# A list scheduler that orders an attention and two-layer MLP kernel: waiting for urgent tasks, later stores and loads, later squares

## The chip, the cores and the metric

The kernel runs on one core of one Trainium2 chip. The metric is the device time of one execution in microseconds (us). A core has TensorE (matrix products; PE in the rows, with PEld for its weight loads), VectorE (DVE), ScalarE (ACT), GpSimd (POOL) and SyncE (SP). Here GpSimd issues the stores of intermediate results, and SyncE issues all loads and the stores of the output. Each engine runs its own instructions strictly in the order in which they were issued to it when the program was built, and waits on semaphores for the others.

## The reference

```python
def reference(q, k, v, phi, moe_w_in, moe_w_out, moe2_w_in, moe2_w_out):
    a = exp(phi - phi.max(2)); a /= a.sum(2) + 1e-9        # 8 batches, 8 heads, 576 tokens, 32 slots
    k_m, v_m = einsum('bhsm,bhsd->bhmd', a, k), einsum('bhsm,bhsd->bhmd', a, v)
    s = q @ k_m.T / sqrt(64); p = exp(s - s.max(-1)); p /= p.sum(-1) + 1e-9
    x = (p @ v_m).transpose(0, 2, 1, 3).reshape(4608, 512)
    h = x @ moe_w_in;  x = (h * sigmoid(h)) @ moe_w_out    # 512 -> 2048 -> 512
    h = x @ moe2_w_in; return where(h > 0, h, exp(min(h, 0)) - 1) @ moe2_w_out
```

All inputs and the output are float32. q, k, v and phi are 8 x 8 x 576 x 64 (phi: x 32).

## The kernel before, in words

A float32 product is made of three float16 products: an operand is split into a high part (`split_hi`, line 170, ScalarE) and a low part (`split_lo`, line 175, VectorE). Products of the two-layer parts use a seven-product scheme for 2 x 2 blocks, so that sums of quarter matrices are formed on VectorE before and after (lines 134 and 1461). Weights arrive as 64-bit words ("raw", 1 MB a load, line 305), are converted in five steps (line 311 on ScalarE, then four on VectorE), split, and written back to memory as float16 (tile `hl_q`, stores `w1os`, `w2is`, `w2os` on GpSimd's queue, lines 444 and 448); later they are read again as `w1s`, `wi` and `wq`.

The program has three parts. The **first**, up to 77 us, is a written-out list (`FIRST`) of the attention of batches 0 and 1. **Plan 1** (`plan_first`, 77 to 718 us) holds the first MLP for batches 0 to 7, with the attention of later batches and the preparation of the second MLP's weights beneath it. In it a batch's silu `h <- ph` (line 1106, ScalarE) follows products `ph <- aT,u`; h is split into `T` and multiplied as `ph <- T,w1s`; `y` is the batch's result, stored to `x2d` (line 1277, 576 KB) and squared and summed by ScalarE (line 354) for a scale. **Plan 2** (718 us to the end) finishes batch 7 and runs the second MLP over 9 blocks of 512 tokens: products `h2A` and `h2D`, ScalarE's copies `h <- h2A` (line 1457), VectorE's additions (line 1461), elu (lines 1492, 1495 and 1499), the split into `t`, and products `o <- t,wq`.

The order inside plan 1 and plan 2 is made by a list scheduler, `Plan`. Each task has an engine, a cost, a rank (lower is more urgent) and dependencies. `run` simulates the engines greedily: the engine that can start earliest takes, of the tasks that are ready by then, the one of lowest rank, and its code is issued at that moment. The costs and the simulated time decide this order and nothing else; on the chip no engine waits for anything but semaphores. In plan 1 the ranks are due times worked out backwards from the products (`by_due`, in us of the planner); in plan 2 they are numbers written by hand, 1000 for each block. `store` gives a GpSimd store a cost of 4.0 + KB/200, and `load` gives a DMA load 3.6 + KB/350 in plan 1 and 2.2 + KB/350 in plan 2, with a term `late` where a caller adds one. `ring` and `take` tell the scheduler which buffers a task must wait for. The raw loads, `hl_q` pairs and scratch tiles share one ring of two buffers, so a raw load or a split can also wait for a store that reads the buffer it wants.

The scheduler's simulation starts a task as soon as nothing ready is more urgent:

```python
start = max(free[eng], min(at[i] for i in r))
i = min((i for i in r if at[i] <= start), key=lambda i: (self.tasks[i][2], i))
```

In plan 2 the last batch's `plan_out1` returns a list `done`, on which the gate for opening the output's PSUM tiles (`open_ps_o`) and the scale of the last batch (`x2_scales(B - 1, NB)` in block 2) both wait.

Of the kernel before, what the change touches and what calls it, by code (L numbers as in the profile page):

```python
# [10 lines left out]
F32 = mybir.dt.float32  # L11
# [8 lines left out]
P = 128  # L20
# [6 lines left out]
HS = S // 2  # L27
# [12 lines left out]
NY = 2  # L40
NT = 3
KVLATE, QLATE = 1.0, 3.0
NKV = 3
W2FROM, W2TO, AHEAD = 0.2, 0.95, 35
SHIFT = 9
# [45 lines left out]
def attn_moe_moe(ctx: ExitStack, tc: tile.TileContext, qT, phiT, kvm, kvt, w1i, w1o, w2i, w2o, out):  # L91
# [96 lines left out]
    class Plan:  # L188
# [47 lines left out]

        def store(self, kb, rank, fn, deps=()):

            return self.add("POOL", 4.0 + kb / 200, rank, fn, deps, 1.2)

        def ring(self, name, n):

# [8 lines left out]
        def run(self):  # L251
            if self.ahead is not None:
                self.by_due()
            n = len(self.tasks)
            left = [len(t[4]) for t in self.tasks]
            users = [[] for _ in range(n)]
            for i, t in enumerate(self.tasks):
                for d in t[4]:
                    users[d].append(i)
            at = [0.0] * n  # L260
            ready = {}
            free = {}
            for i, t in enumerate(self.tasks):
                ready.setdefault(t[0], [])
                free[t[0]] = self.busy.get(t[0], 0.0)
                if not left[i]:
                    ready[t[0]].append(i)
            order = []
            while len(order) < n:
                best = None  # L270
                for eng, r in ready.items():
                    if not r:
                        continue
                    start = max(free[eng], min(at[i] for i in r))
                    i = min((i for i in r if at[i] <= start), key=lambda i: (self.tasks[i][2], i))
                    if best is None or start < best[0]:
                        best = (start, eng, i)
                start, eng, i = best
                ready[eng].remove(i)
                order.append(i)  # L280
                _, cost, _, fn, _, hold = self.tasks[i]
                end = start + cost
                free[eng] = start + hold
                for u in users[i]:
                    at[u] = max(at[u], end + (0.0 if self.tasks[u][0] == eng else COST["wait"]))
                    left[u] -= 1
                    if not left[u]:
                        ready[self.tasks[u][0]].append(u)
                fn()
            return {e: max(0.0, free[e] - free["PE"]) for e in free}  # L290
# [10 lines left out]
    def load64(src, f, s, tag=None):  # L301

        shape = list(src.shape[2:])
        t = (late if tag else two).tile([P, shape[1], shape[2], 2], U32, tag=tag or "raw", name="raw")
        nc.sync.dma_start(out=t.rearrange("p a b w -> p a (b w)"), in_=src[f, s].bitcast(U32))
        raw[id(src), f, s] = t
# [234 lines left out]
    def plan_quads(pl, due, src, e, shape, s_all, n_all, p_all, part, store):  # L541
# [7 lines left out]
        ready, free = {}, {}  # L549
        for k, name in enumerate(order):  # L550
            pl.due = due[k]
            load = pl.load(1024, 0, lambda k=k: load64(src, e, k), pl.ring("raw", 2))
            rfree = pl.take("raw", load)

            def alloc(name=name):
                t[name] = two.tile([P, *shape], F32, tag="stage", name="quad", bufs=4)
                return t[name]

            ready[name] = plan_convert(pl, 0, alloc, src, e, k, [load] + pl.ring("stage", 4))
            free[name] = pl.take("stage", ready[name])  # L560
            rfree.append(ready[name])
# [619 lines left out]
        pl.take("wr", t)  # L1181
        return t

    def plan_out1(pl, b, r, silus, made, stored, scales, y_tile, y_ring):

# [87 lines left out]
        for e in E:  # L1275
            def store(e=e):
                nc.gpsimd.dma_start(out=x2d[b][:, e::2], in_=w[e]["y"].rearrange("p (a t) s -> p a (t s)", a=2))

            def squares(e=e):
                sumsq(mx_x2[:, b, e:e + 1], w[e]["y"], w[e]["y"])  # L1280

            t = pl.store(590, r - 2500, store, [c11[e], c12[e], c21[e], c22[e]])
            yfree[e].append(pl.add("ACT", act(4 * HS), r - 100, squares, [t]))
            done += [yfree[e][-1], c12[e], c21[e], p3[e]]
        return done, [loads[j][0] for j in WSEQ]


    FIRST4, LAST3 = (0, 5, 4, 2), (1, 6, 3)
# [476 lines left out]
    with tc.manual_schedule():  # L1765
# [15 lines left out]
        last["made"] = {}  # L1781
        for n in range(NT):
            last["T_free", n] = pl.take("T", None)
        out1, loads = plan_out1(
            pl, B - 1, 0, None, NT, {}, [], lambda: ph2.tile([P, 4, HS], F32, tag="y", name="y", bufs=2), ("y", 2))
        w1s_load = pl.gates["x"] = loads[4:5]
        pl.gates[1] = [pl.add("PE", 0.0, 0, open_ps_o, out1)]
        for n in range(4, 7):
# [5 lines left out]
        for i in range(NB):  # L1794
            for q in range(KQ):
                plan_in2(pl, i, q)
            plan_out2(pl, i, 0)
            if i == 2:
                pl.add("DVE", 2.5, 1000 * i + RANK["x2"], lambda: x2_scales(B - 1, NB), [y[i]["t_done", KQ - 1, 0]] + out1)
            if i + 1 < NB:  # L1800
                plan_x2(pl, i + 1, 1000 * i + RANK["x2"])
            plan_out2(pl, i, 1)
# [50 lines left out]
```

## Time and profile before

| | us |
|---|---|
| Median of three runs (lowest, highest) | 1409.9 (1408.24, 1411.55) |
| The profiled execution | 1407.48 |
| Its span | 1405.5 |
| TensorE busy with matmuls | 1354.2 (96%) |
| VectorE busy | 1127.9 (80%) |
| ScalarE busy | 951.1 (68%) |
| Mean granted TensorE clock | 0.989 of full speed |

The span runs from the first to the last instruction; the execution takes about 2 us more. Busy shares are means over stages that differ. In a timeline row a bracket such as [3.08 <-ACT pad L178] says how long the engine was idle before the instruction and which work, by engine, tile and line, released it. A name such as SPq or POOLq means the engine's DMA queue. The granted clock is a share of the full 2.4 GHz.

### The profile page before, as it was taken

How to read it: one execution, taken by the hardware profiler on the slowest of the kernel's cores; microseconds unless marked ns; L12 is line 12 of the kernel's file. 1: busy time of each engine (PE TensorE's matmuls, PEld its weight loads, DVE VectorE, ACT ScalarE, POOL GpSimd, SP SyncE). 2: the span in 40 equal slices, each digit the busy share in tenths (PEclk: the TensorE clock that was granted, in tenths of full speed). 3: DMA queues.
4: the chain of work that ended last, by engine and by line, in shares of the span. 5: the costliest groups of instructions: out<-in, count | busy, mean ns of one | idle time of the engine just before them, and what ended most of it. 6: DMA issues, size and time to landing. Idle time of an engine off the chain costs nothing.

```text
span 1405.5 us, 28627 instructions
## 1 busy us (share of the span) xinstructions
PE 1354.2 (96%) x12048; PEld 1092.9 (78%) x12048; DVE 1127.9 (80%) x1753; ACT 951.1 (68%) x1357; POOL 51.1 (4%) x85
## 2 busy tenths in 40 slices
PE   4999999999989999999998999999999999999998
PEld 2667676776756767676786888888888888888887
DVE  6889788796977989797767787887879787878784
ACT  3667765957857596776657576767667676767583
POOL 0001100000010010011000000000000000000000
PEclk8999999999999999999999999999999999999999
DMA  9565767367475657736293233332424151514130
GB/s 363 178 227 176 287 246 255 140 218 278 150 246 197 232 188 253 257 129 224 104 369 132 83 112 107 110 109 84 135 69 151 43 177 43 163 56 136 57 120 31
DMA packets 68801, 233.06 MB, mean 166 GB/s; under 512 B 9025, under 2 KB 15169, under 8 KB 64065
## 3 DMA queue, kind: packets, MB, share of 16 engines
q1 hardware_dynamic: 60288, 199.78, 42.1%
q0 software_dynamic: 8384, 31.46, 5.6%
q8 instruction: 94, 1.54, 0.4%
q14 instruction: 35, 0.28, 0.1%
HBM read 186.12 MB, written 40.89 MB: 162 GB/s over the span
## 4 chain that ended last, share of the span: by engine, by line
PE 79%; DMA 7%; DVE 4%; issue 4%; ACT 4%; POOL 0%; SPq 0%; ACTq 0%; POOLq 0%; DVEq 0%
PE ph L1020 24%; PE o L1020 22%; PE h2A L1020 12%; PE h2D L1020 9%; PE ph L1069 4%; DMA wi<-w2is 3%; PE ph L1027 2%; PE sc L775 2%; PE up L860 2%; PE kvp L679 1%; DMA kv<-in_kvm 1%; DMA x2d<-y 1%; DMA raw<-in_w2i 1%; DMA w2is<-hl_q 1%; DVE T L175 1%
## 5 line engine op out<-in xcount | busy, mean ns | idle before, releaser
L1020 PE MATMUL o<-t,wq 128*128 128x256 f16 x3024 | 361.4, 273 | 1.3 <-DVE t L175 1.3
L1020 PEld LDWEIGHTS <-wi 128*128 128x128 f16 x3024 | 296.2, 98 | 50.1 <-issue 7.2
L1020 PEld LDWEIGHTS <-wq 128*128 128x128 f16 x3024 | 296.1, 98 | 36.3 <-issue 1.7
L1020 PE MATMUL ph<-T,w1s 128*128 128x288 f16 x2352 | 301.9, 286 | 0.0
L1020 PEld LDWEIGHTS <-w1s 128*128 128x128 f16 x2352 | 225.9, 98 | 64.7 <-issue 8.6
L1020 PE MATMUL h2A<-xh,wi 128*128 128x256 f16 x1728 | 228.2, 274 | 10.0 <-ACT h L1457 6.0
L1457 ACT ACTIVATE h<-h2A,inv 128x256 f32<-128x256 f32 x288 | 133.3, 467 | 111.7 <-PE h2A L1020 108.9
L1020 PE MATMUL ph<-aT,u 128*128 128x288 f16 x1344 | 179.8, 290 | 8.8 <-ACT h L1106 8.5
L1020 PEld LDWEIGHTS <-u 128*128 128x128 f16 x1344 | 129.0, 99 | 59.2 <-issue 26.4
L170 ACT ACTIVATE t<-h,s_g 128x768 f16<-128x768 f32 (+1 forms) x144 | 147.4, 1037 | 37.5 <-DVE h L1499 25.9
L1020 PE MATMUL h2D<-xh,wi 128*128 128x256 f16 x1296 | 172.0, 274 | 0.1
L175 DVE SCALAR_TENSOR_TENSOR t<-h,s_g,t 128x768 f16<-128x768 f32 (+1 forms) x144 | 163.4, 1145 | 4.9 <-ACT t L170 4.9
L175 DVE SCALAR_TENSOR_TENSOR T<-h,c,T 128x1152 f16<-128x1152 f32 x98 | 137.2, 1412 | 22.7 <-ACT T L170 22.6
L1461 DVE SCALAR_TENSOR_TENSOR h<-h2D,inv,h 128x256 f32<-128x256 f32 x216 | 102.4, 480 | 65.1 <-PE h2D L1020 43.8
L170 ACT ACTIVATE T<-h,c 128x1152 f16<-128x1152 f32 x98 | 119.9, 1253 | 25.1 <-DVE h L134 19.9
L134 DVE TENSOR_TENSOR h<-h 128x256 f32<-128x256 f32 (+1 forms) x302 | 128.5, 463 | 3.0
L1499 DVE SCALAR_TENSOR_TENSOR h<-e,h 128x1024 f32<-128x1024 f32 x72 | 87.9, 1221 | 20.7 <-ACT e L1495 20.2
L1106 ACT ACTIVATE h<-ph,inv 128x576 f32<-128x576 f32 x112 | 82.1, 737 | 15.9 <-PE ph L1020 15.4
L1492 ACT ACTIVATE e<-h 128x1024 f32<-128x1024 f32 x72 | 75.5, 1048 | 13.7 <-DVE h L1461 13.6
L1495 ACT ACTIVATE e<-e 128x1024 f32<-128x1024 f32 x72 | 75.7, 1051 | 1.0
L1069 PE MATMUL ph<-h,w1o 128*128 128x288 f32 x256 | 66.7, 416 | 0.0
L134 DVE TENSOR_TENSOR h<-h,h 128x1152 f32<-128x1152 f32 x42 | 56.5, 1353 | 7.2 <-ACT h L1106 7.0
(183 smaller groups left out, 1271.2 us busy)
## 6 DMA issues: line engine op xcount, KB each, us to landing
w1s<-w1os SPq DMA_DIRECT2D x98, 512.0 KB, 4.5
wi<-w2is SPq DMA_DIRECT2D x56, 896.0 KB, 4.7
kv<-in_kvm SPq DMA_DIRECT2D x48, 256.0 KB, 5.5
q<-in_qT SPq DMA_DIRECT2D x32, 288.0 KB, 7.3
out<-ye SPq DMA_DIRECT2D x36, 256.0 KB, 2.0
raw<-in_w1i SPq DMA_DIRECT2D x8, 1024.0 KB, 11.5
raw<-in_w1o SPq DMA_DIRECT2D x8, 1024.0 KB, 4.9
raw<-in_w2i SPq DMA_DIRECT2D x8, 1024.0 KB, 6.7
```

What stands on the lines that cost most here:

```text
L134: nc.vector.tensor_tensor(out=out, in0=a, in1=b, op=op)
L170: nc.scalar.activation(out=hi, in_=x, func=AF.Copy, scale=s)
L175: nc.vector.scalar_tensor_tensor(out=lo, in0=x, scalar=s, in1=hi, op0=ALU.mult, op1=ALU.subtract)
L775: nc.tensor.matmul(ps[o:o + 64, c // 2, 2 * p:2 * p + 2], z["q", p][:, t0:t0 + 64], z["kT"][:, p // 2, 64 * (p % 2):64 * (p % 2) + 64], st ...
L1020: nc.tensor.matmul(o, w, x[:, c], start=first, stop=last, **how)
L1069: nc.tensor.matmul(z[d][1][t], wB[d][:, k], h[k // KQ][:, t, k % KQ], start=(k == 0), stop=(k == KF - 1))
L1106: nc.scalar.activation(out=h[m // KQ][:, :, m % KQ], in_=w.pop(m), func=AF.Silu, scale=z["inv1"][:, m // 4:m // 4 + 1])
L1457: nc.scalar.activation(out=w["x"][:, s], in_=w["A"], func=AF.Copy, scale=inv)
L1461: return pl.add("DVE", COST["add"], base, lambda: nc.vector.scalar_tensor_tensor(out=w["x"][:, s], in0=w["D"], scalar=inv, in1=w["x"][:, s ...
L1492: nc.scalar.activation(out=w["e"], in_=w["x"][:, B21:], func=AF.Relu, scale=-1.0)
L1495: nc.scalar.activation(out=w["e"], in_=w["e"], func=AF.Exp, scale=-1.0)
L1499: nc.vector.scalar_tensor_tensor(out=x, in0=w["e"], scalar=-1.0, in1=x, op0=ALU.add, op1=ALU.max)
```

## The change

Three things change, all in the scheduler's numbers and rules; the set of instructions of every engine stays the same, and so does the written-out first part.

1. In `run`, for ScalarE and VectorE, if a task that is more urgent by over 10 (plan 1, us of due time) or over 50 (plan 2, ranks) becomes ready within SOON = 0.4 us of the simulated start, and the task otherwise chosen would still be running 0.2 us past that moment, the engine takes the urgent one and is idle until then. This holds in the simulation. On the chip it only means that the urgent instruction is issued ahead of the other.
2. In plan 1 a store is simulated as 6.0 + KB/200 in place of 4.0 + KB/200, and the raw loads of `plan_quads` (second MLP's weights) land 2.0 us later in the simulation.
3. The squares of the last batch's `y` get rank 1200 in plan 2 (they had -100, ahead of all of the second MLP), no longer stand in `done`, and are waited for only by the scale of the last batch in block 2.

```diff
+RAWLATE, STORE = 2.0, 6.0
+SOON, EARLIER = 0.4, 10.0
...
         def store(self, kb, rank, fn, deps=()):
-            return self.add("POOL", 4.0 + kb / 200, rank, fn, deps, 1.2)
+            return self.add("POOL", (4.0 if self.ahead is None else STORE) + kb / 200, rank, fn, deps, 1.2)
...
                     i = min((i for i in r if at[i] <= start), key=lambda i: (self.tasks[i][2], i))
+                    if eng in ("ACT", "DVE"):
+
+                        rank, end = self.tasks[i][2], start + self.tasks[i][1]
+                        soon = [k for k in r if start < at[k] <= start + SOON and end > at[k] + SOON / 2 and self.tasks[k][2] < rank - (EARLIER if self.ahead is not None else 50)]
+                        if soon:
+                            i = min(soon, key=lambda k: (at[k], k))
+                            start = at[i]
...
-            load = pl.load(1024, 0, lambda k=k: load64(src, e, k), pl.ring("raw", 2))
+            load = pl.load(1024, 0, lambda k=k: load64(src, e, k), pl.ring("raw", 2), RAWLATE)
...
-    def plan_out1(pl, b, r, silus, made, stored, scales, y_tile, y_ring):
+    def plan_out1(pl, b, r, silus, made, stored, scales, y_tile, y_ring, squares_rank=0):
...
-            yfree[e].append(pl.add("ACT", act(4 * HS), r - 100, squares, [t]))
-            done += [yfree[e][-1], c12[e], c21[e], p3[e]]
-        return done, [loads[j][0] for j in WSEQ]
+            yfree[e].append(pl.add("ACT", act(4 * HS), squares_rank, squares, [t]))
+            done += [c12[e], c21[e], p3[e]]
+        return done, [y[-1] for y in yfree], [loads[j][0] for j in WSEQ]
...
-        out1, loads = plan_out1(
-            pl, B - 1, 0, None, NT, {}, [], lambda: ph2.tile([P, 4, HS], F32, tag="y", name="y", bufs=2), ("y", 2))
+        out1, squares, loads = plan_out1(
+            pl, B - 1, 0, None, NT, {}, [], lambda: ph2.tile([P, 4, HS], F32, tag="y", name="y", bufs=2), ("y", 2), 1200)
...
-                pl.add("DVE", 2.5, 1000 * i + RANK["x2"], lambda: x2_scales(B - 1, NB), [y[i]["t_done", KQ - 1, 0]] + out1)
+                pl.add("DVE", 2.5, 1000 * i + RANK["x2"], lambda: x2_scales(B - 1, NB), [y[i]["t_done", KQ - 1, 0]] + squares)
```

Since costs and rules changed, the order of plan 1 and plan 2 is drawn anew from its beginning: TensorE's order is the same up to its 338th matmul, and every engine's order differs after that. Line numbers of the changed kernel are 2 higher from line 42 on and 9 or 10 higher from the scheduler's loop on, so that its lines 172, 320, 363, 1115 and 1467 are lines 170, 311, 354, 1106 and 1457 of before. Three places follow.

**ScalarE in batch 3 of plan 1, at 330 to 343 us of the trace before** (`quad <- raw` is the first step of converting a raw load of the second MLP's weights; `h_145` and `h_146` are silus, each of which frees the PSUM tile of a product). Before:

```order
L1106 ACTIVATE h_145<-ph,inv_3310 128x2x288
L170 ACTIVATE u_3_3217<-up 128x512
L311 ACTIVATE quad<-raw 128x1024
L1106 ACTIVATE h_145<-ph,inv_3310 128x2x288
L354 ACTIVATE y,mx_x_147<-y 128x1152
L1106 ACTIVATE h_145<-ph,inv_3310 128x2x288
L170 ACTIVATE u_3_3159<-up 128x512
L1106 ACTIVATE h_145<-ph,inv_3310 128x2x288
L170 ACTIVATE T<-h_145,c_3312 128x1152
L1106 ACTIVATE h_146<-ph,inv_3310 128x2x288
L311 ACTIVATE quad<-raw 128x1024
```
Of the change, from the same T on:

```order
L172 ACTIVATE T<-h_145,c_3315 128x1152
L1115 ACTIVATE h_145<-ph,inv_3313 128x2x288
L172 ACTIVATE u_3_3210<-up 128x512
L1115 ACTIVATE h_145<-ph,inv_3313 128x2x288
L363 ACTIVATE y,mx_x_147<-y 128x1152
L1115 ACTIVATE h_145<-ph,inv_3313 128x2x288
L172 ACTIVATE u_3_3166<-up 128x512
L320 ACTIVATE quad<-raw 128x1024
L1115 ACTIVATE h_145<-ph,inv_3313 128x2x288
L1115 ACTIVATE h_146<-ph,inv_3313 128x2x288
L172 ACTIVATE u_3_3210<-up 128x512
```
The first conversion moved behind two silus, a square and a split of u. The second (the last row of before) stands seven rows below the end of this piece, behind four more silus.

**ScalarE in batch 4 of plan 1, at 405 to 419 us** (`hl_q <- quad` is the high half of a split; its buffer may be one that a store of an earlier pair still reads). Before, from the load of the silu table on:

```order
L1106 ACT_TABLE_LOAD
L1106 ACTIVATE h_145<-ph,inv_4279 128x2x288
L170 ACTIVATE u_4_4250<-up 128x512
L170 ACTIVATE hl_q<-quad,s_w2i 128x4x256
L1106 ACTIVATE h_145<-ph,inv_4279 128x2x288
L170 ACTIVATE hl_q<-quad,s_w2i 128x4x256
L1106 ACTIVATE h_145<-ph,inv_4279 128x2x288
L170 ACTIVATE u_4_4192<-up 128x512
L170 ACTIVATE hl_q<-quad,s_w2i 128x4x256
L1106 ACTIVATE h_145<-ph,inv_4279 128x2x288 x2
L170 ACTIVATE T<-h_145,c_4281 128x1152
L170 ACTIVATE u_4_4250<-up 128x512
```
Of the change, from the same place:

```order
L1115 ACT_TABLE_LOAD
L1115 ACTIVATE h_145<-ph,inv_4295 128x2x288
L172 ACTIVATE u_4_4243<-up 128x512
L1115 ACTIVATE h_145<-ph,inv_4295 128x2x288
L172 ACTIVATE hl_q<-quad,s_w2i 128x4x256
L1115 ACTIVATE h_145<-ph,inv_4295 128x2x288
L172 ACTIVATE u_4_4198<-up 128x512
L172 ACTIVATE hl_q<-quad,s_w2i 128x4x256
L1115 ACTIVATE h_145<-ph,inv_4295 128x2x288 x2
L172 ACTIVATE u_4_4243<-up 128x512
L172 ACTIVATE T<-h_145,c_4297 128x1152
L1115 ACTIVATE h_145<-ph,inv_4295 128x2x288
L172 ACTIVATE hl_q<-quad,s_w2i 128x4x256
```
One hl_q fewer stands among the first silus, and the third moved behind three silus, a split of u and T.

**ScalarE at the beginning of plan 2, at 733 to 746 us** (`h <- h2A` copies a product out of PSUM, 128x256; the squares are the rows with mx_x). Before:

```order
L170 ACTIVATE t_8261<-h_8133,s_g 128x1024
L1457 ACTIVATE h_8239<-h2A,inv_7712 128x256
L1457 ACTIVATE h_8250<-h2A,inv_7712 128x256
L1457 ACTIVATE h_8239<-h2A,inv_7712 128x256
L1457 ACTIVATE h_8250<-h2A,inv_7712 128x256
L354 ACTIVATE y,mx_x_147<-y 128x1152 x2
L1457 ACTIVATE h_8250<-h2A,inv_7712 128x256
L1457 ACTIVATE h_8366<-h2A,inv_7712 128x256
L1492 ACTIVATE e<-h_8239 128x1024
L1495 ACTIVATE e<-e 128x1024
L1457 ACTIVATE h_8366<-h2A,inv_7712 128x256
```
Of the change, from the same split of t on:

```order
L172 ACTIVATE t_8410<-h_8239,s_g 128x768
L172 ACTIVATE t_8410<-h_8239,s_g 128x1024
L1467 ACTIVATE h_8360<-h2A,inv_7712 128x256
L172 ACTIVATE t_8446<-h_8254,s_g 128x768
L1502 ACTIVATE e<-h_8360 128x1024
L1505 ACTIVATE e<-e 128x1024
L1467 ACTIVATE h_8463<-h2A,inv_7712 128x256
L363 ACTIVATE y,mx_x_147<-y 128x1152
L172 ACTIVATE t_8446<-h_8254,s_g 128x1024
L1467 ACTIVATE h_8463<-h2A,inv_7712 128x256
L363 ACTIVATE y,mx_x_147<-y 128x1152
```
The squares moved from in front of two elu pairs to behind three of them, some fifteen rows later, and the copies of h2A stand ahead of them.

Two other places, in words. At 100 us, the first `kvp <- kvw` of group 1 is sixteen matmuls in a row; in the order of before the second eight wait for ScalarE's copies out of the same PSUM tile (`pad <- kvp` of group 0), and one conversion `w1o <- raw` stands in front of those copies; in the change all sixteen are issued ahead of the copies and wait for none, and the conversion stands behind them. At 433 us, SyncE issues a raw load of w2o ahead of a load `kv <- in_kvm` in the order of before; in the change the kv load stands ahead.

## Rows read from the trace of the kernel before

**Rows 1.** Page: busy time of TensorE's matmuls, share of the span, number of instructions.
```profile
PE 1354.2 (96%) x12048; PEld 1092.9 (78%) x12048; DVE 1127.9 (80%) x1753; ACT 951.1 (68%) x1357; POOL 51.1 (4%) x85
```

**Rows 2.** Waits of TensorE: line waited for, us in total, times, longest us.
```profile
PE ph L1020 <- ACT h L1106: 8.5, 6, 4.3
...
PE h2A L1020 <- DMA wi<-w2is: 3.4, 5, 1.7
```

**Rows 3.** Stretches: length, busy us (instructions) by engine, granted clock, DMA share, GB/s.
```profile
core 0: us, PE busy (x) PEld busy (x) DVE busy (x) ACT busy (x) POOL busy (x), PEclk, DMA share, GB/s
...
100.00:158.00 58.00, 54.92 (x397) 39.25 (x386) 52.05 (x96) 37.63 (x66) 7.27 (x13) 0.97 0.63 204
...
300.00:380.00 80.00, 76.59 (x703) 55.04 (x701) 65.03 (x89) 55.08 (x83) 4.48 (x7) 0.98 0.65 226
380.00:460.00 80.00, 74.35 (x697) 52.86 (x696) 62.53 (x89) 51.23 (x75) 8.51 (x11) 0.96 0.65 224
...
718.00:760.00 42.00, 35.23 (x282) 28.95 (x280) 24.75 (x45) 27.80 (x42) 1.43 (x2) 0.92 0.62 227
...
1078.00:1152.00 74.00, 73.75 (x677) 65.87 (x675) 60.39 (x102) 52.03 (x73) 0.00 (x0) 1.00 0.33 104
```

**Rows 4.** Stretches of TensorE: length, busy us (instructions), clock, DMA share, GB/s.
```profile
104.20:111.00 6.80, 6.76 (x42) 0.75 0.86 305
...
417.40:424.20 6.80, 6.80 (x41) 0.62 0.58 195
...
743.40:746.60 3.20, 3.19 (x16) 0.51 0.04 16
```

**Rows 5.** Timeline at 102 us: start, us, engine, line, tile, count, [idle before <-releaser].
```profile
102.41 1.12 ACT L311 ACTIVATE w1o<-raw 128x1024 f32<-128x1024 f32 x1 [1.20 <-DMA raw<-in_w1o]
...
104.24 0.64 PE L679 MATMUL kvp<-kvw,es 128*32 128x128 f32 x16 [3.08 <-ACT pad L178]
```

**Rows 6.** Timeline of ScalarE at 331 and 341 us.
```profile
331.27 1.12 ACT L311 ACTIVATE quad<-raw 128x1024 f32<-128x1024 f32 x1 [3.11 <-DMA raw<-in_w2i]
...
341.05 1.13 ACT L311 ACTIVATE quad<-raw 128x1024 f32<-128x1024 f32 x1 [2.43 <-DMA raw<-in_w2i]
```

**Rows 7.** Timeline at 406 to 418 us.
```profile
406.67 0.72 POOL L448 DMA_DIRECT2D w2is<-hl_q  x1 [5.30 <-issue]
...
415.57 1.15 ACT L170 ACTIVATE hl_q<-quad,s_w2i 128x1024 f16<-128x1024 f32 x1 [4.23 <-DMA w2is<-hl_q]
...
417.40 3.04 PE L1020 MATMUL ph<-aT,u 128*128 128x288 f16 x12 [4.27 <-ACT h L1106]
```

**Rows 8.** Timeline at 433 to 443 us.
```profile
433.79 0.37 SPq L622 DMA_DIRECT2D kv<-in_kvm  x1
...
442.84 0.43 PE L679 MATMUL kvp<-kv,es 128*32 128x128 f32 x8 [1.34 <-DMA kv<-in_kvm]
```

**Rows 9.** Timeline of TensorE at 656 and 660 us.
```profile
656.38 3.30 PE L1020 MATMUL ph<-aT,u 128*128 128x288 f16 x24 [0.58 <-ACT h L1106]
660.48 0.62 PE L860 MATMUL up<-w1i_hl,vT 128*32 128x512 f16 x8 [0.79 <-DVE u L175]
```

**Rows 10.** Timeline at 737 to 744 us.
```profile
737.93 0.32 SPq L1306 DMA_DIRECT2D wi<-w2is  x1
...
738.75 1.16 ACT L354 ACTIVATE y<-y 128x1152 f32<-128x1152 f32 x1 [3.00 <-DMA x2d<-y]
...
741.38 1.16 ACT L354 ACTIVATE y<-y 128x1152 f32<-128x1152 f32 x1 [1.38 <-DMA x2d<-y]
...
743.41 1.44 PE L1020 MATMUL h2A<-xh,wi 128*128 128x256 f16 x6 [3.88 <-ACT h L1457]
```

**Rows 11.** DMA issues at 406.7, 729.5, 737.9 us: KB, us to landing.
```profile
w2is<-hl_q POOLq DMA_DIRECT2D x1, 512.0 KB, 8.8
x2d<-y POOLq DMA_DIRECT2D x2, 576.0 KB, 10.2
wi<-w2is SPq DMA_DIRECT2D x1, 896.0 KB, 6.9
```

## The prediction

> **What bounds the kernel now.** I read the page's busy line first: TensorE is busy for 1354.2 of 1405.5 us, so all other engines matter only where they make TensorE stand still or lose clock [rows 1]. The whole of what a new order can win is 1405.5 - 1354.2 = 51.3 us of idle time, plus what a lower clock costs. Next I cut the span into stretches and compared length, busy time and clock. A block of plan 2 from 1078 to 1152 us has 73.75 busy of 74 at clock 1.00, so there is nothing to win in it [rows 3]. Four stretches are not full: 100 to 158 us has 58 - 54.92 = 3.1 idle and a clock of 0.97, which costs 0.03 x 58 = 1.7; 300 to 380 has 3.4 idle and 0.02 x 80 = 1.6; 380 to 460 has 5.65 and 0.04 x 80 = 3.2; 718 to 760 has 6.8 and 0.08 x 42 = 3.4 [rows 3]. That is 19 us idle and 10 us of clock, about 29 in all. The written-out first part, up to 77 us, stays as it is. The list of TensorE's waits says for whom it waits: 8.5 us for silus on ScalarE in six waits, the longest 4.3 [rows 2]. Last I opened the timeline at each of these waits, and asked what the releasing engine was itself waiting for. In all the large ones it is the same: an instruction that waits for a DMA stands on ScalarE ahead of one that TensorE needs, though the needed one could have run. ScalarE is in order, so it is held up by what was put ahead of it.
>
> The clock falls behind such waits. After the wait that ends at 104.2 us the next 6.8 us run at 0.75; after the one that ends at 417.4, 6.8 us at 0.62; after the one that ends at 743.4, 3.2 us at 0.51, nearly the lower level of 1.2 GHz [rows 4]. So a wait is paid about one and a half times.
>
> **The change part by part.** It removes and adds no instruction, so no duration changes; it is costed by the waits that the new order removes and makes. The idling that the new rule speaks of exists in the planner alone and costs the chip nothing by itself.
>
> a) At 102 us ScalarE waits 1.2 us for a raw load, converts for 1.12, and only then copies the pads, for which TensorE waits 3.08 us [rows 5]. In the new order the matmuls wait for no pads, and the conversion stands behind the first pads. Idle 3.1 and clock 0.25 x 6.8 = 1.7 go [rows 4, 5]: **4.8 us**.
>
> b) At 331 and 341 us ScalarE waits 3.11 and 2.43 us for raw loads of w2i with silus behind them [rows 6]. In the new order two silus, a square and a split stand ahead of the first conversion, and each silu stands for twelve matmuls, so some 3.3 us of products [rows 9]: the load has landed or nearly so. The second is four silus later. What the stretch loses is 3.4 idle and 1.6 clock [rows 3]; of these 5.0 I take **4.6 us**, since a stretch so long keeps a little idle time. The bound below is 2.4, about the half: the second load waits for the buffer that the first conversion frees, and may slip with it.
>
> c) At 415.57 us ScalarE has waited 4.23 us for a store that was issued at 406.67 and took 8.8 us to land, and TensorE waits 4.27 us for the silu behind [rows 7, 11]. In the new order this split stands three silus, a split of u and T later, which is 3 x 1.65 + 0.62 = 5.6 us of products [rows 9], more than the 4.23 that it was short. Idle 4.27 and clock 0.38 x 6.8 = 2.6 go [rows 4, 7]: **6.9 us**. The planner reckoned the store at 4.0 + 512/200 = 6.6 us and now reckons 8.6, so for stores like this one its view becomes right. Bound below: 3.0, if the store starts later too, as GpSimd then has a store of y ahead of the pair's second store.
>
> The Trainium skill ("DMA: Bandwidth & Descriptors", section "Anatomy of one DMA — SWDGE (gpsimd) path") puts a GpSimd transfer at about 2.0 us plus bytes over 436 GB/s, an estimate of 3.2 us for 512 KB. The trace does not agree here: this store took 8.8 us [rows 11]. If the rule held in this stretch, neither the old nor the new cost would be too short, the term c would be nothing, and the time would be 6.9 us more than forecast, about 1400.
>
> d) At 442.84 us TensorE waits 1.34 us for a kv load that was issued at 433.79, behind a raw load [rows 8]. Now it stands ahead: **1.3 us**.
>
> e) At 656 and 660 us TensorE waits 0.58 for a silu and 0.79 for a split of u [rows 9]. Now the silu and u stand ahead of the splits of weights: **1.4 us**.
>
> f) At 738.75 and 741.38 us the squares wait 3.00 and 1.38 us for their stores, which took 10.2 us in the median, and TensorE's 3.88 us wait for a copy of h2A is behind them [rows 10, 11]. In the new order the squares come some fifteen ScalarE instructions later. If nothing else bound there, all 6.8 + 3.4 = 10.2 us of this stretch would go [rows 3]. But a load of wi was issued at 737.93 and took 6.9 us, that is to 744.8, and TensorE needs that tile soon after [rows 10, 11]; in plan 2 TensorE already waits 3.4 us for such loads [rows 2]. A load that starts when its buffer comes free, some 4 to 6 us of products ahead of its use, and lands 6.9 us later, leaves 1 to 3 us of wait, and a clock behind it as in rows 4. I take **4.0 us**, bounds 0 and 10.2.
>
> Sum of what goes: 4.8 + 4.6 + 6.9 + 1.3 + 1.4 + 4.0 = 23.0.
>
> g) What comes. All of plan 1 and plan 2 is drawn anew, so new small waits are to be expected. The trace of before cannot show them. From below they cost 0; from above as much as plan 1's waits of before cost together, the first three stretches above with 12.2 idle and 6.5 clock = 18.7 us [rows 3]. The planner now allows for late stores and late raw loads, which made the three large ones, so I take what the smaller kinds cost before: 0.58, 0.79 and 1.34 [rows 8, 9], as many again elsewhere (2.7), and 0.6 of clock: **6.0 us**. Places that I would look at: batch 1 near 129 us, where its vT now stands behind squares of the weights on ScalarE, and the copies of h2A in plan 2's first block.
>
> In plan 2's blocks the 50-rank rule holds VectorE and ScalarE back in the planner. VectorE is busy for 60.39 of 74 us a block, so 13.6 us are free [rows 3]: costed at nothing, covered by that room.
>
> Net: 23.0 - 6.0 = 17.0. The profiled execution took 1407.5 us; minus 17.0 gives 1390.5. It lay 2.4 under the median of the three runs, so the median should be 1409.9 - 17 = **1393**.
>
> **The rivals.**
> - *The squares give nothing (f = 0).* The load of wi and the traffic around it hold TensorE in place of the squares. For: 0.62 DMA share over that whole stretch [rows 3], and 6.9 us for wi against 4 to 6 us of room. Against: from 738.75 - 3.00 = 735.75 to 742.5 ScalarE does nothing but wait for and run the squares [rows 10]. Time: 1397.
> - *New waits eat most of it.* They come to the upper bound of g, 18.7 instead of 6.0: 1393 + 12.7 = 1406; with b and c at their lower bounds, too, 1393 + 12.7 + 2.2 + 3.9 = 1412, no change. For: a due-time order is sensitive, and the stores' landing varies widely. Against: both modelled delays move towards what the rows show.
> - *Slower: lo splits come late in plan 2.* If VectorE's low halves of t are issued behind additions that come later on the chip than in the plan, TensorE's `o <- t,wq` wait in each block. At 3 us a block over 8 blocks that is 24 us: 1393 + 24 = 1417. It decides from 2.1 us a block on (17/8). Against: 13.6 us of free VectorE time a block [rows 3].
> - *All is recovered.* f gives 10.2 and nothing new comes: 1393 - 6.2 - 6.0 = 1381.
>
> **How the numbers follow.** My forecast (1386 to 1400) 0.58; squares give nothing 0.15; new waits eat most 0.15, of which 0.05 still faster, 0.08 within the bound and 0.02 slower; slower by plan 2 0.05; all recovered 0.07. A measurement here tells 0.2%, 2.8 us, from no change. Faster: 0.58 + 0.15 + 0.07 + 0.05 = 0.85; same 0.08; slower 0.02 + 0.05 = 0.07. The range leaves out about half of "all recovered" and the slow half of "new waits" and the slower rival: 1383 to 1406.
>
> **What would show it.** In the changed kernel's stretches 300 to 380 and 380 to 460 should have under 1.5 us idle each and a clock of 0.99 or more, and TensorE's waits for silus (8.5 us now) should fall under 3. ScalarE's conversions and splits should show no bracket over 1 us for a raw load or a store with a TensorE wait behind it. At 738 us the copies of h2A should run on, and if f is right in size a wait of 1 to 3 us for wi stands there. The blocks of plan 2 should keep 73.7 of 74. I am wrong if long waits for a DMA stand ahead of silus at other places, or if the blocks of plan 2 grow.

## The result

The changed kernel takes 1390.55 us (median of four executions, 1388.78 to 1393.87); before took 1409.52 beside it. The ratio is 0.9867, 95% interval 0.9842 to 0.9892, so the change is 1.3% faster. Forecast were 1393 and a range of 1383 to 1406. The profiled execution took 1392.21 us, its span 1390.1: 15.4 us less than before.

The page, busy line (beside [rows 1]):

```profile
PE 1345.9 (97%) x12048; PEld 1091.0 (78%) x12048; DVE 1130.3 (81%) x1753; ACT 948.2 (68%) x1357; POOL 53.2 (4%) x85
```

TensorE has 1390.1 - 1345.9 = 44.2 us idle where it had 51.3, and is busy 8.3 us less with the same matmuls. Of 15.4 us, then, 7.1 are idle time and 8.3 busy time. The mean granted clock rose from 0.989 to 0.992, which is 0.011 x 1405.5 - 0.008 x 1390.1 = 4.3 us of the busy time; for the rest the page has no row (it models where a matmul ends).

TensorE's waits in the changed kernel, largest of plan 1 and 2 (beside [rows 2]; us in total, times, longest):

```profile
PE h2A L1029 <- DMA wi<-w2is: 7.4, 7, 1.4
...
PE kvTp L753 <- ACT pad L180: 4.4, 3, 3.5
PE kvp L688 <- DMA kv<-in_kvm: 4.2, 3, 2.5
PE h2A L1029 <- ACT h L1467: 1.5, 3, 0.6
...
PE ph L1029 <- ACT h L1115: 0.9, 2, 0.7
```

Of before, the rows that [rows 2] does not show:

```profile
PE h2A L1020 <- ACT h L1457: 6.0, 5, 3.9
...
PE kvp L679 <- DMA kv<-in_kvm: 1.9, 2, 1.3
...
PE kvTp L744 <- ACT pad L178: 0.9, 2, 0.7
```

The waits for silus fell from 8.5 to 0.9, and those for copies of h2A from 6.0 to 1.5. In their place stand longer waits for pads (kvTp), for kv loads and for wi: what is late next.

The same stretches as in [rows 3] (the fourth starts at 711, as plan 2 starts 9 us earlier):

```profile
core 0: us, PE busy (x), PEclk, DMA share, GB/s
100.00:158.00 58.00, 54.55 (x370) 0.94 0.70 221
300.00:380.00 80.00, 77.35 (x713) 0.98 0.69 237
380.00:460.00 80.00, 78.93 (x753) 1.00 0.67 234
711.00:760.00 49.00, 45.88 (x407) 1.00 0.67 241
1078.00:1152.00 74.00, 72.98 (x670) 1.00 0.32 104
```

380 to 460 us went from 74.35 busy at 0.96 to 78.93 at 1.00. The beginning of plan 2 has 3.1 idle at full clock where it had 6.8 at 0.92. But 100 to 158 us is no better (54.55 at 0.94, was 54.92 at 0.97), and 300 to 380 has 2.65 idle where it had 3.4, at the same clock of 0.98.

A second reading separates the two plans without any window: the row of the h2A matmuls in the view of tile wi gives the start of its first and of its last matmul (behind the three durations in ns). Before:

```profile
L1020 PE MATMUL h2A<-xh,wi x1728: 269/273/421, 718.0 to 1373.0; 128*128 128x256 f16 x192
```

Of the change:

```profile
L1029 PE MATMUL h2A<-xh,wi x1728: 269/273/284, 709.2 to 1356.9; 128*128 128x256 f16 x192
```

Plan 2 starts 718.0 - 709.2 = 8.8 us earlier, and from its first to its last h2A it takes 647.7 us where it took 655.0: 7.3 us less. I use both numbers for every run below. Each is of one execution: a second profile of the change has 708.1 and 646.8, and two profiles with one order of plan 1 (runs 2 and 9) start plan 2 4.6 us apart.

**Where the wait for pads went.** Timeline of the changed kernel at 107 us:

```profile
106.89 1.12 ACT L320 ACTIVATE w1o<-raw 128x1024 f32<-128x1024 f32 x1 [2.87 <-DMA raw<-in_w1o]
...
107.90 0.51 ACT L180 ACTIVATE pad<-kvp,rp 128x64 f32<-128x64 f32 x2
...
108.72 1.11 PE L753 MATMUL kvTp<-ident,pad 128*128 128x128 f32 x4 [3.45 <-ACT pad L180]
```

The conversion still waits for its raw load, 2.87 us, and now it stands ahead of the second group's pads. TensorE's wait of 3.08 us for the first pads [rows 5] became one of 3.45 us for the second.

**Where the waits for raw loads went.** Timeline of the changed kernel at 331 and 336 us:

```profile
326.05 0.44 SPq L631 DMA_DIRECT2D kv<-in_kvm  x1
...
331.41 1.13 ACT L320 ACTIVATE quad<-raw 128x1024 f32<-128x1024 f32 x1 [0.29 <-DMA raw<-in_w2i]
...
336.46 0.66 PE L688 MATMUL kvp<-kv,es 128*32 128x128 f32 x8 [2.47 <-DMA kv<-in_kvm]
```

The conversion waits 0.29 us, not 3.11 [rows 6], and no silu is held up. But TensorE comes 3.8 us earlier to the products with kv, whose load was issued at 326.05 and lands at 336.4, and waits 2.47 us there. Before, the same load was issued at 325.95 and landed 10.3 us later, at 336.3, and TensorE, held up by then, came to it at 337.77 without a wait.

What was late there is not the transfer of the raw load. The chain of work that ended last, in the trace of before (start, us, work):

```profile
317.64 7.22 DMA w2is<-hl_q
325.05 6.19 DMA raw<-in_w2i
...
336.17 4.86 DMA raw<-in_w2i
```

The two raw loads took 6.2 and 4.9 us from issue to landing, and the planner of before already reckons 3.6 + 1024/350 = 6.5 us for one. They were issued late. A raw load can wait for a store that reads the buffer it wants, and each of these was issued within 0.2 us of the landing of a store of `hl_q`: the one issued at 317.64, which took 7.2 us, and the one issued at 327.11, which took 9.0, where the planner reckoned 6.6. The kv load stands behind the first raw load in SyncE's order, so the same store holds it up, in the change as before (the store issued at 317.40 takes 7.6 us there, the raw load follows at 325.18, the kv load at 326.05).

**The beginning of plan 2.** Timeline of the changed kernel, 734 to 743 us (beside [rows 10]):

```profile
734.94 0.83 PE L1029 MATMUL h2A<-xh,wi 128*128 128x256 f16 x6 [0.57 <-DMA wi<-w2is]
...
738.20 1.15 ACT L363 ACTIVATE y<-y 128x1152 f32<-128x1152 f32 x1
...
738.35 0.82 PE L1029 MATMUL h2A<-xh,wi 128*128 128x256 f16 x6 [0.57 <-ACT h L1467]
...
740.74 1.15 ACT L363 ACTIVATE y<-y 128x1152 f32<-128x1152 f32 x1
```

The squares run without a wait, behind the landing of their stores. The wait for wi that was feared is 0.57 us.

### The profile page after: what moved, and what is told of

It reads as the page before. It is cut to its first block, busy times and chain, and to the rows that moved or that the text cites. A ratio compares the mean times of both kernels' runs of the same rounds, so it can differ in the third digit from the quotient of the medians.

```text
span 1390.1 us, 28629 instructions
## 1 busy us (share of the span) xinstructions
PE 1345.9 (97%) x12048; PEld 1091.0 (78%) x12048; DVE 1130.3 (81%) x1753; ACT 948.2 (68%) x1357; POOL 53.2 (4%) x85
## 4 chain that ended last, share of the span: by engine, by line
PE 84%; DMA 5%; issue 4%; DVE 3%; ACT 3%; POOL 0%; SPq 0%; ACTq 0%; POOLq 0%; DVEq 0%
PE ph L1029 28%; PE o L1029 23%; PE h2A L1029 13%; PE h2D L1029 9%; PE ph L1078 3%; DMA wi<-w2is 2%; PE up L869 2%; PE ph L1036 2%; PE sc L784 2%; PE kvp L688 1%; DMA kv<-in_kvm 1%; DMA w2is<-hl_q 1%; PE eT L665 0%; DMA raw<-in_w1o 0%; PE aTp L836 0%
## 5 line engine op out<-in xcount | busy, mean ns | idle before, releaser
L1029 PE MATMUL ph<-aT,u 128*128 128x288 f16 x1344 | 176.5, 288 | 1.1 <-ACT h L1115 0.9
L172 ACT ACTIVATE t<-h,s_g 128x768 f16<-128x768 f32 (+1 forms) x144 | 146.4, 1034 | 22.8 <-DVE h L136 11.5
L172 ACT ACTIVATE T<-h,c 128x1152 f16<-128x1152 f32 x98 | 119.5, 1252 | 13.8 <-DVE h L136 10.3
```

Of the source, the lines that this page charges most:

```text
L172: nc.scalar.activation(out=hi, in_=x, func=AF.Copy, scale=s)
L1029: nc.tensor.matmul(o, w, x[:, c], start=first, stop=last, **how)
```

## The experiments

Every run is timed beside the kernel before. The last two columns are from the row of h2A in each profile.

| run | median us | ratio to before, 95% interval | plan 2 starts | first to last h2A |
|---|---|---|---|---|
| before | 1409.5 | | 718.0 | 655.0 |
| the change | 1390.55 | 0.9867 (0.9842, 0.9892) | 709.2 | 647.7 |
| squares alone | 1406.24 | 0.9975 (0.9956, 0.9994) | 717.2 | 653.5 |
| later stores and loads alone | 1407.47 | 0.9981 (0.9965, 0.9998) | 713.7 | 655.7 |
| waiting rule alone | 1402.81 | 0.9948 (0.9926, 0.9970) | 713.0 | 656.3 |
| change, w1o loads later | 1387.76 | 0.9833 (0.9809, 0.9857) | 705.9 | 646.2 |
| change, rule in plan 1 only | 1397.28 | 0.9896 (0.9871, 0.9921) | 709.5 | 653.5 |
| squares, plan 2's stores later | 1401.61 | 0.9937 (0.9919, 0.9955) | 719.2 | 648.7 |
| change without the squares | 1401.38 | 0.9932 (0.9913, 0.9950) | 709.3 | 656.4 |
| change, w1o and wi later | 1390.73 | 0.9875 (0.9836, 0.9913) | 713.5 | 652.6 |
| change without the rule | 1404.72 | 0.9970 (0.9955, 0.9986) | 718.3 | 656.6 |
| change, again | 1390.47 | 0.9856 (0.9844, 0.9869) | 708.1 | 646.8 |
| change, w1o loads later, again | 1390.56 | 0.9854 (0.9837, 0.9870) | 707.9 | 647.2 |
| change, w1o and kv loads later | 1401.57 | 0.9948 (0.9931, 0.9965) | 719.4 | 647.1 |

**1. The squares alone**: before with

```diff
-            yfree[e].append(pl.add("ACT", act(4 * HS), r - 100, squares, [t]))
-            done += [yfree[e][-1], c12[e], c21[e], p3[e]]
+            yfree[e].append(pl.add("ACT", act(4 * HS), squares_rank, squares, [t]))
+            done += [c12[e], c21[e], p3[e]]
```

and the scale of the last batch waiting for the squares, as in the change.

> The kernel before with the squares of the last batch moved alone. Theory (each part has its own place): plan 1 is as before, the first h2A of plan 2 starts near 718 us as before, and the 6.8 us idle and 3.4 us of clock of the stretch from 718 to 760 fall to about 3 idle at full clock, so some 7 us less: 1402.5. Rival (the load of wi binds there anyway): 1405 to 1409, and a wait for wi of 2 to 4 us stands where the squares did.

Measured 1406.24, 0.25% faster; plan 2 is 1.5 us shorter, not 7. The time is inside the rival's range, but no wait of 2 to 4 us for wi stands there. Neither theory holds as put. The timeline at the beginning of plan 2:

```profile
738.54 1.16 ACT L354 ACTIVATE y<-y 128x1152 f32<-128x1152 f32 x1 [3.59 <-DMA x2d<-y]
...
741.52 0.81 PE L1020 MATMUL h2A<-xh,wi 128*128 128x256 f16 x6 [2.82 <-ACT h L1457]
```

The first square, at its low rank, still waits 3.59 us for its store, and TensorE 2.82 us for the copy of h2A behind it. The planner has the store landed after 4.0 + 590/200 = 7.0 us, sees ScalarE free and starts the square, whatever its rank. The store took 9.8 us from issue to landing.

**2. Later stores and loads alone**: before with

```diff
+            return self.add("POOL", (4.0 if self.ahead is None else STORE) + kb / 200, rank, fn, deps, 1.2)
...
+            load = pl.load(1024, 0, lambda k=k: load64(src, e, k), pl.ring("raw", 2), RAWLATE)
```

> The kernel before with the later modelled stores and raw loads alone. Theory (the large waits of plan 1 come from the planner taking stores and loads for too early): TensorE's waits for silus fall from 8.5 to under 3 us, plan 2 starts 5 to 8 us earlier, and the squares still cost what they did: 1403. Rival (the rule to wait for urgent tasks puts the silus ahead): the silus still wait 6 us or more, time 1408 to 1412.

```profile
PE ph L1022 <- ACT h L1108: 2.4, 5, 0.6
```

The waits for silus fell from 8.5 to 2.4 us, as the theory said, and in this profile plan 2 starts 4.3 us earlier. The median gained only 2.6 us, so the time is 4.5 us over the theory's. The profiled execution (1404.05) is the fastest of the ten, and run 9, with the same order through plan 1, starts plan 2 at 718.3: the 4.3 us are not a safe measure of what these costs win by themselves. A new wait of 3.35 us near 130 us (for the attention weights of batch 1, on VectorE) takes part of it back.

**3. The waiting rule alone**: before with the eight lines of the rule in `run`.

> The kernel before with the rule to wait for a more urgent task alone. Theory (late stores and loads): no large wait goes, since each was made by a DMA that came 2 us or more later than planned and not by a task that was ready within 0.4 us: 1406 to 1411. Rival (the rule does it): plan 2 starts 5 us or more earlier, 1400 to 1404.

Measured 1402.81, and plan 2 starts 5.0 us earlier: the rival is right. By the medians the rule alone wins 7.3 us, and the later costs alone 2.6. The theory's reason is half right. ScalarE's timeline in this run:

```profile
334.04 1.12 ACT L320 ACTIVATE quad<-raw 128x1024 f32<-128x1024 f32 x1 [4.33 <-DMA raw<-in_w2i]
...
343.67 1.12 ACT L320 ACTIVATE quad<-raw 128x1024 f32<-128x1024 f32 x1 [3.46 <-DMA raw<-in_w2i]
...
417.40 1.15 ACT L172 ACTIVATE hl_q<-quad,s_w2i 128x1024 f16<-128x1024 f32 x1
```

At 334 and 344 us the conversions still wait 4.33 and 3.46 us for raw loads, with TensorE behind them (3.24 and 2.72 us); in the second run, with the later stores and raw loads, neither waits. At 417 us the split of w2i does not wait any more, though the stores here are modelled as early as before: the order drawn anew put it behind its store's landing, as it does in the second run.

**4. The raw loads of w1o modelled later as well** (and once more, beside the change): the change with

```diff
-                load = pl.load(1024, 3, lambda d=d, s=s: load64(w1o, d, s), pl.ring("raw", 2))
+                load = pl.load(1024, 3, lambda d=d, s=s: load64(w1o, d, s), pl.ring("raw", 2), RAWLATE)
```

> The changed kernel, with the raw loads of w1o in plan 1 modelled 2.0 us later too. In its order all six copies of pads stand ahead of the conversion that waits for the raw load at 104 us. Theory (the 3.45 us wait of the transposes of the pads and the half clock behind it come from that conversion): the wait goes and the clock from 100 to 158 us rises from 0.94 to near 1.00, so 3.4 + 3.4 = 6 to 7 us less than the changed kernel: 1384. Rival (the wait only moves again, as it did from before to the change): 1389 to 1392, and another wait of 2 us or more stands between 100 and 158 us.

The wait of the transposes of pads is gone: TensorE's wait for pads in kvTp is 0.9 us (4.4 in the change), and one of 1.0 at the kvp matmuls remains. Measured 1387.76 at 0.9833. Since the change had 0.9867 in another comparison, I ran both beside each other:

> The changed kernel again, beside the next two on one chip. Every theory: 1388 to 1393.

> The changed kernel with the raw loads of w1o modelled 2.0 us later, as in the fourth run. Theory (the wait for the pads at 104 us is gone): 3 us less than the changed kernel beside it. Rival (the difference seen was between chips or executions): within 1 us of it.

The change 1390.47, this 1390.56: the rival is right, no difference is measured here, though the wait is gone in both profiles. The two profiles differ in two stretches (length, busy, clock, DMA share, GB/s). The change, again:

```profile
100.00:184.00 84.00, 79.51 (x617) 0.98 0.79 257
330.00:360.00 30.00, 28.57 (x258) 1.00 0.70 251
```

With the w1o loads later:

```profile
100.00:184.00 84.00, 82.26 (x668) 1.00 0.74 248
330.00:360.00 30.00, 27.43 (x234) 0.94 0.64 235
```

From 100 to 184 us it wins 2.75 us of idle time and 1.7 of clock. From 330 to 360 it loses 1.1 and 1.8 again. The wait there, for kv, is

```profile
324.85 0.44 SPq L631 DMA_DIRECT2D kv<-in_kvm  x1
...
335.00 0.65 PE L688 MATMUL kvp<-kv,es 128*32 128x128 f32 x8 [2.56 <-DMA kv<-in_kvm]
```

The kv load is issued 1.4 us earlier than in the other run (324.85, there 326.27) and takes 10.1 us, so TensorE, which comes 3 us earlier, waits 2.56 us in place of 1.43.

That the edit itself moved the wait is not shown by this. The first profile of the change, without the edit, has the longer wait too (2.47 us) and the same clock:

```profile
330.00:360.00 30.00, 27.53 (x239) 0.94 0.66 238
```

And the fourth run, with 2.92 us of this wait, took 1387.42. With four executions of each, a gain between nothing and some 3 us stays open.

**5. The rule in plan 1 only**: the change with

```diff
-... and self.tasks[k][2] < rank - (EARLIER if self.ahead is not None else 50)]
+... and self.tasks[k][2] < rank - EARLIER and self.ahead is not None]
```

> The changed kernel with the rule to wait for a more urgent task switched off in plan 2; the order of plan 1 is the same to the last silu of it. Theory (the rule takes half of the gain at the beginning of plan 2, since it puts copies of h2A ahead of the squares): plan 2 starts as in the changed kernel, near 709 us, its second block starts 3 to 4 us later than there, and a square waits for its store again: 1394. Rival (the moved squares did it alone): 1390 to 1391, and the same start of the second block, near 781.

Plan 1 as in the change (709.5), plan 2 5.8 us longer, 1397.28: the theory holds and is a little small. A square waits for its store again:

```profile
730.70 1.16 ACT L363 ACTIVATE y<-y 128x1152 f32<-128x1152 f32 x1 [3.48 <-DMA x2d<-y]
...
733.68 0.82 PE L1029 MATMUL h2A<-xh,wi 128*128 128x256 f16 x6 [2.71 <-ACT h L1467]
```

**6. The squares, with plan 2's two stores modelled later**: the first run with

```diff
-            return self.add("POOL", 4.0 + kb / 200, rank, fn, deps, 1.2)
+            return self.add("POOL", (4.0 if self.ahead is not None else 8.0) + kb / 200, rank, fn, deps, 1.2)
```

> The kernel before with the squares moved, and the two stores of plan 2 modelled as 8.0 + KB/200 us in place of 4.0. In its order the first square stands eight rows of ScalarE later than with the squares moved alone. Theory (a low rank is not enough: the planner still starts the first square when it believes the store landed, 3 us too early): no square waits for its store, the 2.8 us wait for a copy of h2A goes, and the second block starts 3 to 5 us earlier than with the squares alone: 1402. Rival (something else binds in this stretch, the load of wi): 1405 to 1407, and a wait of 2 us or more for wi.

Plan 2 takes 648.7 us, 6.3 less than before and 4.8 less than with the squares alone, with no waiting rule at all: 1401.61. The squares run at 743.9 and 747.8 us without a wait, and the longest wait left there is one of 1.21 for wi. The theory holds.

**7. The change without the squares**: items 1 and 2 of the change, the squares as before.

> The changed kernel with the squares of the last batch back in their old place. Theory: plan 1 is the changed kernel's, its start of plan 2 near 709 us; the wait for the squares (4 us and the clock behind it) is back, 7 us more than the changed kernel: 1397.5. Rival (the rule already keeps the squares out of the way): 1391 to 1393.

Plan 1 as in the change (709.3), plan 2 656.4, that is 8.7 us longer: 1401.38, above what the theory gave. ScalarE waits 4.14 and 1.61 us for the two stores, and TensorE 5.3 us for the copy of h2A behind them:

```profile
730.50 1.16 ACT L363 ACTIVATE y<-y 128x1152 f32<-128x1152 f32 x1 [4.14 <-DMA x2d<-y]
...
735.40 1.44 PE L1029 MATMUL h2A<-xh,wi 128*128 128x256 f16 x6 [5.30 <-ACT h L1467]
```

The rule alone does nothing for plan 2.

**8. The loads of wi modelled later**: the fourth run with

```diff
-            wi_load[q] = pl.load(896, base, lambda: load_wi(q, "wi"), pl.ring("wi", NRING))
+            wi_load[q] = pl.load(896, base, lambda: load_wi(q, "wi"), pl.ring("wi", NRING), 1.2)
```

> The changed kernel with the raw loads of w1o modelled 2.0 us later (as in the fourth run) and the loads of wi in the blocks of plan 2 modelled 1.2 us later. Theory (the waits of 1.0 to 1.6 us for wi, one a block in five blocks of the changed kernel, come from a load that lands about a us later than the plan has it): these waits fall under 2 us in all, 4 us less than the fourth run: 1384. Rival (the two buffers of wi set the distance, and the plan has no other work to put in between): 1387 to 1389, and as much wait elsewhere in the block.

The waits for wi fell to 2.3 us, and yet plan 2 takes 652.6 us in this profile, 6.4 more than in the fourth run's; the median is 3.0 us above that run's, and 0.2 above the fourth run's kernel in its second timing (1390.56). TensorE's waits in plan 2:

```profile
PE h2A L1029 <- ACT h L1467: 5.4, 18, 0.6
...
PE h2A L1029 <- DMA wi<-w2is: 2.3, 2, 1.6
```

Eighteen small waits for copies of h2A stand where the fourth run has three, and two for wi in place of six. The theory falls, since the time did not fall with the waits for wi. Why plan 2 is longer is not shown: it is idle for 9.4 us where the fourth run's is idle for 7.8, which is 1.6 of the 6.4, and the profiled execution took 1400.7 us where the other three took 1389.2 to 1392.2.

**9. The change without the rule**: items 2 and 3 alone.

> The changed kernel without the rule to wait for a more urgent task; later stores, loads and squares stay. Theory (the parts do not add up: without the rule a square waits for its store again at the beginning of plan 2, and plan 1 is the one of the second run): plan 2 starts near 713 us, as with the later stores and loads alone, and the time is 1402 to 1405. Rival (the later costs and squares are the change, the rule is a detail): 1391 to 1394.

Measured 1404.72: 14 us above the change. The theory holds in the time and in the square: plan 2 takes 656.6 us, and its first square waits 3.19 us for its store. Plan 2 starts at 718.3, not near 713, in a profiled execution of 1409.4, which is 4.7 over the median of its ten. Later costs and squares together win 5.9 us over before, and alone they won 2.6 and 3.9: these two parts add up.

**10. The kv loads modelled later too**: the fourth run with

```diff
-KVLATE, QLATE = 1.0, 3.0
+KVLATE, QLATE = 4.0, 3.0
```

> As the run before this one, with the kv loads modelled 3.0 us later too. Theory (the waits of 2.9 and 1.0 us for kv come from loads that land later than planned, as the raw loads did): TensorE's waits for kv fall from 3.8 to under 1.5 us and the time by 2 to 3 us: 1384 to 1385. Rival (the kv ring of three buffers and the queue set the landing, and the attention chain gets late): 1387 to 1391, with waits of the same size at other places.

TensorE no longer waits for kv at all, and plan 2 starts 11.5 us later than in the run beside it: 1401.57. The rival is right in its mechanism; its time of 1387 to 1391 was 10 us too short. The waits moved along the attention's chain:

```profile
PE up L869 <- DVE u L177: 5.4, 5, 1.9
...
PE aTp L836 <- DVE att L136: 5.3, 6, 2.4
PE ph L1029 <- ACT h L1115: 3.0, 5, 0.7
```

## Why the prediction was right, point by point

The sum was 17.0 us and the medians differ by 19.0; the profiled spans differ by 15.4. Its terms were not all right, and errors cancel: plan 1 was to win 19.0 us less the new waits and won 8.8, plan 2 was to win 4.0 and won 7.3. That the total came so near is in part luck.

- **What bounds the kernel** holds: the large waits were instructions that wait for a DMA, ahead of one that TensorE needs. Runs 1, 3, 5 and 7 show it, each with such an instruction back in the way.
- **a) 4.8 us: this step failed.** I saw that the matmuls of kvp no longer wait and that the first pads stand ahead of the conversion, and took that for the end of the wait. The second pads still stand behind it, the transposes need both, and the wait is 3.45 us. In run 4 it goes, which shows that the conversion is its cause. Where 4.8 us were to be won, the stretch from 100 to 158 us lost 0.4 more of idle time and 1.7 of clock.
- **b) 4.6 us, bound below 2.4:** that the conversions stop waiting is right (run 2 has no such wait, run 3 has it, so the later stores and raw loads remove it; which of the two was not tried apart). What made the raw loads late was not their own time, 6.2 and 4.9 us, but the stores that they wait for, 7.2 and 9.0. The size is wrong, and below the bound: the kv load that before was hidden by the stall comes into view at 2.47 us, so the idle time fell by 0.76 us and the clock stayed at 0.98.
- **c) 6.9, d) 1.3:** the stretch from 380 to 460 us, where the work itself now stands up to 8 us earlier, gained 4.58 of idle time and its clock went from 0.96 to 1.00, worth 3.2: 7.8 together, where c and d were 8.2. Right in size. The cause that I gave for c, that a store's cost becomes right, is not needed: with the rule alone the wait is gone as well (run 3). Which of the later stores and the later raw loads does it in run 2 was not tried apart.
- **e) 1.4:** the stretch from 620 to 681 us has 60.31 busy, where it had 59.38: 0.9. The wait for u is gone. That for the silu is not, 0.69 us at 648.13, though a split of weights no longer stands ahead of it: the silu starts when ScalarE's load of its table (646.05, 1.28 us) ends.
- **f) 4.0, bounds 0 and 10.2:** mis-sized; plan 2 gained 7.3. Of these 2.3 are idle time (11.36 us before, 9.04 in the change) and 5.0 busy time, of which the clock of the first stretch, 0.92 before and 1.00 in the change, is 3.4. The wait for wi that I set against it is 0.57 us. What decides the term is whether a square stands behind the landing of its store, 10.3 us after its issue in the median of the two. A low rank is not enough (run 1: 1.5 us); it needs the waiting rule (the change, 7.3) or a later modelled store (run 6, 6.3).
- **The rule in plan 2, costed at nothing:** wrong. With the squares in their old place it is worth nothing or less (656.4 and 656.3 us, before 655.0), with them moved it is worth 5.8 (run 5). The two parts cannot be added: 1.5 and -1.4 alone, 7.3 together. Rule and squares without the later costs were not run.
- **g) 6.0 of new waits:** they came near this size, but not at the places named under g: waits for kv, 4.2 us where they were 1.9, and for wi in the blocks, 7.4 where they were 3.4, so 6.3 more together (the pads are counted under a). The stretch from 1078 to 1152 us has 72.98 busy, 0.8 less than before.
- **The rivals:** "the squares give nothing" is nearly what the moved squares do alone, and so stands and falls with the rule, or with a later modelled store (run 6). New waits came, but far from the bound of 18.7. The slower rival did not come: TensorE waits nowhere 3 us in a block.
- **The signs:** two came, silus at 0.9 us and 380 to 460 us with 1.07 idle at 1.00. Four did not: 300 to 380 us has 2.65 idle at 0.98, a conversion still waits 2.87 us for a raw load with TensorE behind it, the wait for wi near 738 us is 0.57, and the block has 72.98 of 74.

## What to carry to other kernels

Where a scheduler's model sets an in-order queue, look first for instructions that wait for a DMA and ask whether the modelled landing is earlier than the real one; lowering the rank of such an instruction does little if the model believes that it is ready. Then ask whether the transfer is slow or was issued late: here two raw loads kept to their modelled time and stood behind late stores. When a stall is removed, read what else was late under it: here a kv load, and the second group behind the same conversion, took a good part back. Parts of a scheduling change need not add up (3.9, 2.6 and 7.3 us alone, 13.8, against 19 together): the rule in plan 2 loses 1.4 us alone and wins 5.8 with the squares, so a part that does nothing alone may be needed. And a transfer modelled later may cost more than it saves (run 10, 11 us).

## What the runs showed of the hardware that was not expected

The fourth and the eighth run have the same order of instructions on every engine into the first block of plan 2, and yet their profiled executions, on two chips, start plan 2 at 705.9 and 713.5 us. One raw load of w1o, issued at 99.3 and at 98.5 us behind the same transfers, took 7.6 us in the one and 11.8 in the other, and the next 5.7 and 8.5; TensorE then waits 3.4 us at 131 us in the slower one. Why these loads were slower stays open. So executions of one order differ by as much as some of the parts measured here, and the other three of the eighth run took 1389.2 to 1392.2 against this one's 1400.7.

The kv load (256 KB) that is issued near 326 us behind a raw load took 10.1 to 10.6 us from issue to landing in four profiles, at a DMA share of about 0.8, where the median of all kv loads of before is 5.5. In a quieter stretch (428.3 to 431.7 us of the changed kernel, DMA share 0.44) the same kind of store that took 8.8 us before [rows 11], at a share of 0.98, took 3.3 (512 KB, issued at 428.33). That is near what the Trainium skill's formula gives ("DMA: Bandwidth & Descriptors", section "Anatomy of one DMA — SWDGE (gpsimd) path": an estimate of 3.2). All such stores of the changed kernel took 2.9 to 9.6 us, 4.8 in the median; so by this trace the formula is near the lower end, and a planner that took it for the landing would take many stores as landed too early. That the traffic is the reason is not shown: no run changed it alone.
